# Kernel values of a long convolution written out by group of 32 partitions and gathered in 1-KB runs, in a two-part kernel on one core

## The chip, the core and the metric

The kernel runs on one core of a Trainium2 chip. The metric is the device time of one execution in microseconds (us). Three executions of the kernel before took 1983.52, 1980.21 and 1974.15 us, a median of 1980.21 us. The engines are called as the profile calls them: PE is TensorE, DVE is VectorE, ACT is ScalarE, POOL is GpSimd and SP is SyncE, which here does nothing but issue transfers.

## The reference, cut to what is computed

Two independent computations share the launch; their outputs lie side by side.

```python
# A: attention over 64 segments of 32 rows; 8 memory rows are handed from segment to segment
for s in range(64):
    h = concat([mem, x[32*s:32*s+32]])             # 40 rows of 1024
    q, k, v = h@Wq, h@Wk, h@Wv                     # 32 heads of 128
    o = softmax(mask(q k^T / sqrt(128))) v @ Wo
    mem, out_a[s] = o[:8], o[8:]
# B: a convolution of length 2048 for each of 1024 channels d
K[d, l] = Re sum_n C[d,n] dt[d] B[d,n] exp(dt[d] (A_re + i A_im)[d,n] l)    # 128 states n
y = irfft(rfft(u, 4096) * rfft(K, 4096))[:2048] + u * Dskip
```

Part B needs the kernel values K[d, l] of each channel, then their spectrum, the product with the spectrum of u, and the way back.

## The kernel before, in words

The function `part_b` runs first and `part_a` after it. The order of the work is written by hand (`manual_schedule`): instructions stand on each engine in the order in which the Python code calls them, and an engine waits only for what an instruction needs. Transfers issued from SP and from ACT are counted on eight completion counters in turn, so a transfer also waits until the one eight places ahead of it in the program has landed.

Part B has these stages.

- **Tables, about 65 to 400 us.** Sixteen rounds `f`, each with the same list of words (`ORDER`). A round makes powers of the states on PE, ACT and DVE (`exp_`, `sine`, `products`), multiplies them into kernel values (`values`), and copies these into a tile `KxT` of 128 partitions, 49 columns and 128 channels (`part_out`). Partition 32g+q holds a coarse place q of channel group g, so one channel's values are spread over 32 partitions. Eight rounds fill one half of the 1024 channels (a half has 512, in four groups of 128). Between these words stand pieces of other work: the transform of u on PE, whose result is written to a DRAM tensor `Ud`, and part A's projections of its left rows (`kst` to `PKd`, `vst` to `PVd`, weights into `wsl`). `kst` is one buffer: when its 16 pieces are filled it is written out in eight transfers (L211), and ACT may fill it again (L206) only after that.
- **Rearranging.** The spectrum needs the values as five tiles of 128 places by 512 channels (`ks`). The first half goes from `KxT` to a DRAM tensor `Kd` in 44 transfers (L1079), each of one channel group and one piece of the table `PLACED`. They wait in the list `late`, and `exp_` issues one each time it is called. `load_k` (L1112) loads the five tiles from `Kd` in two transfers in round 15. The second half goes to `Kx1` in one transfer (L1075), at the end of the table stage. It is rearranged by the generator `load_second`: 12 loads straight into the tile `k1` (L1102), 32 copies from DRAM to DRAM into `Kd1` (L1105), and one load of `Kd1` (L1108).
- **Spectra and the way back, about 400 to 620 us.** Sixteen steps `b`, one for each of four frequency blocks of four channel quarters. Step b calls in this order: `times_u(b)` on DVE (four products, L1394); `load_u(b+1)` on SP (two loads of 512 KB from `Ud` into one pair of buffers, L1229, possible only when `times_u(b)` has read them); `spectrum(b+1)` on PE (40 matmuls, L1238), in two halves of 20 into three buffers `hps`; `rotate` and the sums into `Bt` on DVE; one to three loads of weights for part A (L266); in steps 3 to 6 up to twelve transfers of `load_second` each; from step 4 on two inverses on PE (65 matmuls, L1519 and L1513), with an evacuation on ACT (L1534), a store from ACT's queue (L1541) and a load of u (L1477). `spectrum(8)`, called in step 7, is the first to need the second half's tiles in `k1`. An inverse sums two blocks of 256 columns in one PSUM bank, each opened by its own start flag.

Part A then streams weights that do not fit into SBUF (`wst<-WD_...`) through 64 segments.

The few lines around the change that the text needs:

```python
    for _ in range({1: 2, 2: 2, 3: 1, 4: 2, 5: 2, 6: 2, 7: 1, 11: 3, ...}.get(b, 0)):
        next(resident)                       # weights of part A, 512 KB each
    for _ in range(12 if 2 < b < 7 else 0):
        next(second, None)                   # twelve transfers of load_second
    ...
    if b >= 4:
        inverses(2)
```

Of the kernel before, what the change touches and what calls it, by code (L numbers as in the profile page):

```python
# [10 lines left out]
BF16 = mybir.dt.bfloat16  # L11
# [674 lines left out]
NF = NP + NN  # L686
# [16 lines left out]
def part_b(ctx, tc, u, A_re, A_im, B_re, B_im, C_re, C_im, log_dt, Dskip, out_b, ahead, copies, residents, first_state):  # L703
    nc = tc.nc
    L, D = u.shape
# [3 lines left out]
    DH, DQ = 512, 256  # L709
    v, sc, gp, pe, sy = nc.vector, nc.scalar, nc.gpsimd, nc.tensor, nc.sync  # L710

    const = ctx.enter_context(tc.tile_pool(name="b_const", bufs=1))
    dram = ctx.enter_context(tc.tile_pool(name="b_dram", bufs=1, space=bass.MemoryType.DRAM))
    PB = [dram.tile([PARTS[q], D, 128], BF16, name="PB%d" % q) for q in range(2)]
    Ud = dram.tile([4, 4, 128, 4, 2, DQ], F32, name="Ud")
    Kd = dram.tile([641, DH], BF16, name="Kd")
    Kx1 = dram.tile([128, NF * 128], BF16, name="Kx1")
    Kd1 = dram.tile([256, DH], BF16, name="Kd1")
    MId = dram.tile([16, 128, 2, 4, 128], BF16, name="MId")

    ident = const.tile([128, 128], BF16, name="b_ident")
# [7 lines left out]
    XT = ahead.XM_  # L729
# [39 lines left out]
    with tc.tile_pool(name="b_par", bufs=1) as par, tc.tile_pool(name="b_parh", bufs=2) as parh, \  # L769
# [35 lines left out]
        o = 0  # L805
# [154 lines left out]
        for word_ in PAR:  # L960
            word = word_.rstrip("/")
            nm, n_ = word[0], word[1:]
# [83 lines left out]
    KxT = {}  # L1046
# [12 lines left out]
    def part_out(sb, h, kp):  # L1059
# [4 lines left out]
        if sb % 8 == 7 and h == 1:  # L1064
            put_values(sb)

    late = []

    PLACED = ((0, 0, ((8, 1, 32),)), (8, 256, ((8, 2, 16),)), (16, 384, ((4, 1, 4), (8, 4, 8), (40, 1, 4))),
              (24, 512, ((0, 1, 4), (4, 2, 2), (8, 8, 4), (40, 2, 2), (44, 1, 4))))  # L1070

    def put_values(sb):
        kx = KxT["t"]
        if sb // 8:
            late.append(lambda: sy.dma_start(out=Kx1[:], in_=kx[:].rearrange("p j c -> p (j c)")))  # L1075
            return

        def put(out, in_):
            late.append(lambda: sy.dma_start(out=out, in_=in_))  # L1079
        for g in range(4):  # L1080
            dsl = slice(128 * g, 128 * g + 128)
            for p0, u0, cols in PLACED:
                n_j = sum(n for _, _, n in cols)
                dst = Kd[u0:u0 + 8 * n_j, dsl].rearrange("(i j) d -> i j d", j=n_j)
                at = 0
                for j0, js, n in cols:
                    put(dst[:, at:at + n], kx[32 * g + p0:32 * g + p0 + 8, j0:j0 + js * (n - 1) + 1:js, :])
                    at += n
            put(Kd[640:641, dsl], kx[32 * g + 31:32 * g + 32, NF - 1, :])

    def load_second(KT):
        rows = Kx1[:].rearrange("p (j c) -> p j c", j=NF)
        for g in range(4):
            for p0, u0, cols in PLACED:
                n_j = sum(n for _, _, n in cols)
                at, p = 0, 32 * g + p0
                for j0, js, n in cols:
                    src_ = rows[p:p + 8, j0:j0 + js * (n - 1) + 1:js, :]
                    if len(cols) == 1:
                        for lo in range(0, 8 * n_j, 128):  # L1100
                            o = DH * ((u0 + lo) // 128) + 128 * g
                            sy.dma_start(out=KT[:, o:o + 128], in_=src_[lo // n_j:(lo + 128) // n_j])  # L1102
                            yield
                    else:
                        sy.dma_start(out=Kd1[u0 - 384:u0 - 384 + 8 * n_j, 128 * g:128 * g + 128].rearrange("(i j) d -> i j d", j=n_j)[:, at:at + n], in_=src_)  # L1105
                        yield
                    at += n
        sy.dma_start(out=KT[:, 3 * DH:5 * DH].rearrange("p (j d) -> p j d", j=2), in_=Kd1[:].rearrange("(j p) d -> p j d", p=128))  # L1108
# [118 lines left out]
    def load_u(b):  # L1227
        for n_ in range(2):
            sy.dma_start(out=uq[n_], in_=Ud[b % 4, b // 4][:, 2 * n_:2 * n_ + 2].rearrange("p a c d -> p (a c d)"))  # L1229
# [109 lines left out]
    for f in range(16):  # L1339
        if f == 8:  # L1340
            sy.dma_start(out=Dsk[:], in_=Dskip.partition_broadcast(128))
        ahead.burst = 3 if f == 0 else 2
        if f == 0:
            next(others)
        if 1 <= f <= 6:
            next(steps)
        if f == 15:
            for kind, slot in [k for k in pending if k[0] == "P"]:
                run_evict(kind, slot, v.tensor_copy)
            while ahead.late and ahead.late[0]:  # L1350
# [5 lines left out]
            ks = [load_k(XT[:, 0:2048], 0) + load_k(XT[:, 4096:4608], 4)]  # L1356
# [96 lines left out]
    k1 = pool.tile([128, 4096], BF16, name="k1", tag="KT0")  # L1453
# [53 lines left out]
    def products_back(yp, dq, c, neg, mn, kcs):  # L1507
        r, Bt = c // 4, Bs[dq]
        j = r % 2
        for b in range(2):  # L1510
            for kc in kcs:
                if kc == 3 and b == 1 and c % 4 == 2:
                    pe.matmul(yp[:, b, :], lhsT=l4[:, r, :], rhs=w4[:, DQ * dq:DQ * dq + DQ], start=False, stop=False, skip_group_check=True)  # L1513
                for cs in range(2):

                    g_cs = cs if j == 0 else 1 - cs
                    minus = neg is not None and neg[0] <= cs < neg[1]
                    for half, m_, c_ in ((0, MI[c // 2], cs), (1, mn if minus else MI[c // 2], g_cs)):
                        pe.matmul(yp[:, b, :], lhsT=m_[:, b, cs, kc, :], rhs=Bt[:, kc, j, half, c_, :], start=(kc == 0 and cs == 0 and half == 0),  # L1519
                                  stop=(kc == 3 and cs == 1 and half == 1), skip_group_check=True)  # L1520

    def inverse(dq, c, uu, neg, mn):
# [32 lines left out]
    for b in range(16):  # L1555
# [29 lines left out]
            for i in (2 * b, 2 * b + 1):  # L1585
                sy.dma_start(out=MI[i][:], in_=MId[2 * i:2 * i + 2].rearrange("c p a k q -> p c a k q"))
        if b == 2:
            ks.append([k1[:, DH * j:DH * j + DH] for j in range(5)])
            second = load_second(k1[:, 0:2560])
            rows4 = g0[0:4, 5120:6144]  # L1590
            for i in range(4):
                sy.dma_start(out=rows4[i:i + 1, 0:DH], in_=Kd[640:641, :])
                sy.dma_start(out=rows4[i:i + 1, DH:D].rearrange("o (g c) -> o g c", g=4),
                             in_=Kx1[:].rearrange("(g q) f -> q g f", g=4)[31:32, :, 128 * NF - 128:])
            sy.dma_start(out=w4, in_=u[0:4, :])
            gp.tensor_tensor(out=w4, in0=rows4[:, 0:D], in1=w4, op=ALU.mult)
            gp.memset(l4, 0.0)
            gp.memset(l4[:, :, 127:128], float(PLEN / 2))
            gp.affine_select(out=l4[:, :, 127:128], in_=l4[:, :, 127:128], compare_op=ALU.is_ge, fill=0.0, base=0, pattern=[[1, 4], [0, 1]],
                             channel_multiplier=-1)  # L1600
        for _ in range({1: 2, 2: 2, 3: 1, 4: 2, 5: 2, 6: 2, 7: 1, 11: 3, 12: 3, 13: 2, 14: 3}.get(b, 0)):
            next(resident)
        for _ in range(12 if 2 < b < 7 else 0):
            next(second, None)
        if b == 4:
            state = first_state(g0[0:8, 5120:6144], iv.tile([128, 8, 24], BF16, name="xt0", bufs=1))
            next(state)
# [170 lines left out]
```

## Time and profile before

| What | Value |
|---|---|
| Median of three executions | 1980.21 us |
| The profiled execution | 1981.69 us |
| Its span, first to last instruction | 1979.9 us |
| PE busy | 1840.5 us, 93% of the span |
| DVE busy | 1371.1 us, 69% |
| ACT busy | 949.7 us, 48% |
| Mean granted clock of PE | 0.977 |
| Moved by all transfers | 589.91 MB, 298 GB/s on average |

A busy row of the page is a sum over stages that differ: what a change in one stage is worth is read in that stage. The views used here are the page's 40 slices, tables of busy time by stretch of the span (microseconds from the start; "DMA" is the mean busy share of the 16 DMA engines), and the instructions in order of time. In that last view a row gives the start, the duration, the engine, the line, the operation with output and input, and in brackets the idle time of the engine ahead of it and what ended it. "SPq" and "ACTq" rows are the time that a queue needed to issue a transfer, waits for buffers and counters included, and not the transfer itself.

### The profile page before, as it was taken

What the parts mean: (1) busy time and instruction counts of PE and PEld (TensorE: products, weight loads), DVE (VectorE), ACT (ScalarE), POOL (GpSimd) and SP (SyncE); (2) the same over time, 40 slices, a digit from 0 to 9 for tenths busy, and PEclk for the clock granted to TensorE, in tenths of its full rate; (3) what the DMA queues carried; (4) which work ended last, traced back from release to release, by engine and by line L of the source; (5) the groups of instructions that cost most, each with busy time, mean ns of one, the idle gap of its engine ahead of it and who ended that gap; (6) DMA issues with size and microseconds to landing.
All of it is one profiled execution on the core that took longest, in us unless ns stands there. A gap on an engine that the chain in (4) does not pass through costs nothing.

```text
span 1979.9 us, 74693 instructions
## 1 busy us (share of the span) xinstructions
PE 1840.5 (93%) x32006; PEld 1133.3 (57%) x32044; DVE 1371.1 (69%) x3401; ACT 949.7 (48%) x1678; POOL 389.8 (20%) x823
## 2 busy tenths in 40 slices
PE   8999999787998799999999999999999999999999
PEld 3666566456786455555555555555555555555554
DVE  8699999787893466666666666767666666666650
ACT  8799999832123344434444444444434343434330
POOL 2354454212000111111111111111111111111120
PEclk9999999779999799999999999999999999999999
DMA  7989888765478899999999999999999999999991
GB/s 221 255 238 265 264 239 251 210 223 185 144 250 298 312 338 336 351 333 339 340 338 333 348 347 345 350 339 349 340 336 341 337 344 338 344 342 348 328 344 37
DMA packets 329728, 589.91 MB, mean 298 GB/s; under 512 B 87812, under 2 KB 203368, under 8 KB 327220
## 3 DMA queue, kind: packets, MB, share of 16 engines
q1 hardware_dynamic: 277208, 530.64, 78.4%
q10 hardware_dynamic: 45532, 29.57, 4.9%
q0 software_dynamic: 6656, 24.92, 3.4%
q8 instruction: 251, 4.11, 0.9%
q14 instruction: 81, 0.66, 0.1%
HBM read 528.52 MB, written 67.26 MB: 301 GB/s over the span
## 4 chain that ended last, share of the span: by engine, by line
PE 40%; DMA 22%; DVE 3%; ACT 1%; issue 1%; POOL 0%; ACTq 0%; SPq 0%; POOLq 0%; DVEq 0%
PE acc L408 23%; DMA wst<-WD_o 8%; PE pp L521 8%; DMA wst<-WD_v 6%; DMA wst<-WD_k 3%; PE pe L658 3%; PE tr L419 2%; DMA arena<-PKd 2%; DMA wst<-WD_q 1%; DMA out_dram<-arena 1%; PE pv L489 1%; DVE arena L615 1%; PE pv L493 1%; PE sc L433 1%; ACT arena L615 1%
## 5 line engine op out<-in xcount | busy, mean ns | idle before, releaser
L408 PEld LDWEIGHTS <-a_hT 128*32 128x32 bf16 x12352 | 328.2, 96 | 308.8 <-issue 54.0
L414 ACT CAST arena<-acc 128x512 bf16<-128x512 f32 x384 | 225.1, 586 | 395.0 <-PE acc L408 317.6
L521 PEld LDWEIGHTS <-arena 128*32 128x32 bf16 x8256 | 217.0, 96 | 91.0 <-issue 66.4
L408 PE MATMUL acc<-wst,a_hT 128*32 128x512 bf16 x2304 | 229.4, 381 | 24.1 <-DMA wst<-WD_v 16.4
L422 POOL COPY arena<-arena 128x128 bf16<-128x128 bf16 x128 | 37.3, 292 | 842.5 <-DMA arena<-PKd 274.0
L329 DVE TENSOR_SCALAR arena<-keep 128x256 int32<-128x256 int32 (+1 forms) x512 | 175.7, 395 | 31.5 <-PE acc L408 29.1
L408 PE MATMUL acc<-XM,a_hT 128*32 128x512 bf16 x2560 | 185.9, 380 | 0.0
L521 PE MATMUL pp<-W_o,arena 128*32 128x256 bf16 x3584 | 122.6, 274 | 7.3 <-DMA W_o<-in_A_Wo_dram 7.3
L452 ACT ACTIVATE sc<-sc 128x160 f32<-128x160 f32 (+1 forms) x192 | 63.9, 333 | 126.0 <-DVE sc L449 125.5
L448 DVE TENSOR_REDUCE a_mx<-sc 128x4 f32<-128x160 f32 (+1 forms) x192 | 71.7, 373 | 75.0 <-PE sc L436 75.0
L197 PE MATMUL pro<-XM,wsl 128*128 128x512 bf16 x480 | 117.4, 382 | 5.9 <-DVE kst L206 2.2
L408 PE MATMUL acc<-W,a_hT 128*32 128x512 bf16 x1536 | 119.3, 382 | 0.2 <-issue 0.2
L536 DVE COPY arena<-tr 128x512 bf16<-128x512 bf16 x64 | 27.2, 425 | 126.2 <-PE tr L419 126.2
L456 DVE TENSOR_REDUCE a_mx<-sc 128x4 f32<-128x160 f32 (+1 forms) x192 | 72.9, 379 | 55.4 <-ACT sc L452 55.0
L1519 PE MATMUL yp<-Bt,MI 128*128 128x256 bf16 x680 | 105.2, 274 | 0.0
L408 PE MATMUL acc<-g,a_hT 128*32 128x512 bf16 x1024 | 102.2, 381 | 0.0
L1283 DVE TENSOR_SCALAR nr<-ptt 128x456 f32<-128x456 int16 x128 | 80.3, 628 | 29.8 <-PE ptt L1261 26.9
L483 POOL TENSOR_TENSOR arena<-arena,a_BD 128x128 bf16<-128x128 bf16 x128 | 51.0, 399 | 237.8 <-DVE arena L466 222.8
L615 ACT CAST arena<-pp 128x128 bf16<-128x128 f32 x64 | 17.0, 266 | 164.9 <-DVE arena L615 164.9
L1275 ACT ACTIVATE E<-pa 128x648 bf16<-128x648 f32 x128 | 87.8, 713 | 15.8 <-PE pa L1267 13.9
L521 PE MATMUL pp<-wst,arena 128*32 128x256 bf16 x1536 | 76.6, 275 | 19.3 <-DMA wst<-WD_o 17.4
L408 PE MATMUL acc<-wq,a_hT 128*32 128x512 bf16 x1024 | 91.2, 382 | 0.0
(333 smaller groups left out, 4024.4 us busy)
## 6 DMA issues: line engine op xcount, KB each, us to landing
wst<-WD_v SPq DMA_DIRECT2D x256, 512.0 KB
wst<-WD_k SPq DMA_DIRECT2D x192, 512.0 KB
wst<-WD_o SPq DMA_DIRECT2D x192, 512.0 KB
wst<-WD_q SPq DMA_DIRECT2D x128, 512.0 KB
Ud<-ux POOLq DMA_DIRECT2D x16, 1024.0 KB, 8.2
wq<-Ud SPq DMA_DIRECT2D x32, 512.0 KB
wsl<-in_A_Wk_dram SPq DMA_DIRECT2D x16, 512.0 KB
wsl<-in_A_Wv_dram SPq DMA_DIRECT2D x16, 512.0 KB
```

The source lines that it names most:

```text
L197: nc.tensor.matmul(a[:], lhsT=w[:, kc, 128 * j:128 * j + 128], rhs=xTl[:, kc, :, :].rearrange("p s k -> p (s k)"), start=(kc == 0), stop=( ...
L329: nc.vector.tensor_scalar(out=out.bitcast(I32), in0=in_.bitcast(I32), scalar1=0, scalar2=None, op0=ALU.bitwise_or)
L408: nc.tensor.matmul(a[32 * g:32 * g + 32, o_:o_ + rhs.shape[1]], lhsT=hT[:, kc, :], rhs=rhs, start=(kc == 0), stop=(kc == KC - 1), tile_pos ...
L414: nc.scalar.copy(out=q, in_=a[:])
L448: nc.vector.tensor_reduce(out=m_, in_=x, axis=AX.X, op=ALU.max)
L452: nc.scalar.activation(out=flat(sc, i), in_=flat(sc, i), func=ACT.Exp, scale=scale)
L456: nc.vector.tensor_reduce(out=m_, in_=x, axis=AX.X, op=ALU.add)
L521: nc.tensor.matmul(po[32 * qt:32 * qt + 32, o_:o_ + rhs.shape[1]], lhsT=oT[:, h % 4, (h % 16) // 4, :], rhs=rhs, start=False, stop=(h == 3 ...
L658: nc.tensor.matmul(pe[n][:], lhsT=left[2 * b + hi // 16][:, 128 * (hi % 16):128 * (hi % 16) + 128], rhs=wo[u][:, 1024 * hh + 512 * n:1024 ...
L1275: sc.activation(out=T["E", r, e // 4][:, lo:lo + 8 * NE].rearrange("p (i c) -> p i c", i=2), in_=T.pop(("p", r, e))[:, :, 0:4 * NE], func= ...
L1283: v.tensor_scalar(out=T["n", r, e // 4][:, lo:lo + 8 * NT], in0=T.pop(("t", r, e))[:, 0:8 * NT].bitcast(I16)[:, 0:16 * NT:2], scalar1=floa ...
L1519: pe.matmul(yp[:, b, :], lhsT=m_[:, b, cs, kc, :], rhs=Bt[:, kc, j, half, c_, :], start=(kc == 0 and cs == 0 and half == 0), stop=(kc == 3 ...
```

## The change

Both halves now take the same way. A tile `Kx[half]` in DRAM holds 32 places, 49 columns, 4 groups and 128 channels, so that the four groups of one place and column stand side by side as 512 channels (1 KB). `put_values` writes `KxT` there in four transfers, one for each group of 32 partitions (1568 runs of 256 bytes each). Eight copies a half then put the two irregular pieces into a small tensor `Kp[half]`; the first half's are listed in `late` behind 16 empty entries, the second half's in `second`, four issued in step 3 and four in step 4. `load_k` loads each of the five tiles with a transfer of its own, in runs of 1 KB: three straight from `Kx` (32 columns of four places, twice, and every second column of eight places) and two from `Kp`. It is called in round 15 for the first half and in step 6 for the second. The rows of the last place come from `Kx` for both halves. In the inverse only the first block of a bank has a start flag.

In the built program SP issues 58 transfers fewer (34 for both halves in place of 92); the other engines have the same instructions in the same order.

```diff
-    Kd = dram.tile([641, DH], BF16, name="Kd")
-    Kx1 = dram.tile([128, NF * 128], BF16, name="Kx1")
-    Kd1 = dram.tile([256, DH], BF16, name="Kd1")
+    Kx = [dram.tile([32, NF, 4, 128], BF16, name="Kx%d" % i) for i in range(2)]
+    Kp = [dram.tile([16, 16, DH], BF16, name="Kp%d" % i) for i in range(2)]
...
-    PLACED = ((0, 0, ((8, 1, 32),)), (8, 256, ((8, 2, 16),)), (16, 384, ((4, 1, 4), (8, 4, 8), (40, 1, 4))),
-              (24, 512, ((0, 1, 4), (4, 2, 2), (8, 8, 4), (40, 2, 2), (44, 1, 4))))
+    PIECES = ((16, ((4, 1, 4), (8, 4, 8), (40, 1, 4))), (24, ((0, 1, 4), (4, 2, 2), (8, 8, 4), (40, 2, 2), (44, 1, 4))))
     def put_values(sb):
-        kx = KxT["t"]
-        if sb // 8:
-            late.append(lambda: sy.dma_start(out=Kx1[:], in_=kx[:].rearrange("p j c -> p (j c)")))
-            return
...
+        kx, half = KxT["t"], sb // 8
         for g in range(4):
...
+            late.append(lambda g=g: sy.dma_start(out=Kx[half][:, :, g, :], in_=kx[32 * g:32 * g + 32, :, :]))
+        late.extend([lambda: None] * (16 if half == 0 else 0))
+        for p0, cols in PIECES:
+            at = 0
+            for j0, js, n in cols:
+                (late if half == 0 else second).append(lambda p0=p0, at=at, j0=j0, js=js, n=n: sy.dma_start(
+                    out=Kp[half][p0 - 16:p0 - 8, at:at + n, :],
+                    in_=Kx[half][p0:p0 + 8, j0:j0 + js * (n - 1) + 1:js].rearrange("i j g c -> i j (g c)")))
+                at += n
-    def load_second(KT):
...
-    def load_k(KT, lo):
+    def load_k(half, KT, lo):
         n_ = KT.shape[1] // DH
-        sy.dma_start(out=KT.rearrange("p (j d) -> p j d", j=n_), in_=Kd[128 * lo:128 * (lo + n_), :].rearrange("(j p) d -> p j d", p=128))
-        return [KT[:, DH * j:DH * j + DH] for j in range(n_)]
+        ks_ = [KT[:, DH * j:DH * j + DH] for j in range(n_)]
+        for j, t_ in enumerate(ks_):
+            c = lo + j
+            src_ = Kp[half][8 * (c - 3):8 * (c - 2)] if c > 2 else Kx[half][4 * c:4 * c + 4, 8:40] if c < 2 else Kx[half][8:16, 8:40:2]
+            sy.dma_start(out=t_, in_=src_ if c > 2 else src_.rearrange("i j g c -> i j (g c)"))
+        return ks_
...
-                        pe.matmul(..., start=(kc == 0 and cs == 0 and half == 0),
+                        pe.matmul(..., start=(b == 0 and kc == 0 and cs == 0 and half == 0),
...
-        for _ in range(12 if 2 < b < 7 else 0):
-            next(second, None)
+        for _ in range(4 if b in (3, 4) else 0):
+            second.pop(0)()
+        if b == 6:
+            ks.append(load_k(1, k1[:, 0:2560], 0))
```

More of the change, by code (lines that the diff above doesn't have):

```diff
@@ L1065, in part_out @@
             put_values(sb)
-    late = []
-    PLACED = ((0, 0, ((8, 1, 32),)), (8, 256, ((8, 2, 16),)), (16, 384, ((4, 1, 4), (8, 4, 8), (40, 1, 4))),
-              (24, 512, ((0, 1, 4), (4, 2, 2), (8, 8, 4), (40, 2, 2), (44, 1, 4))))
+    late, second = [], []
+    PIECES = ((16, ((4, 1, 4), (8, 4, 8), (40, 1, 4))), (24, ((0, 1, 4), (4, 2, 2), (8, 8, 4), (40, 2, 2), (44, 1, 4))))
     def put_values(sb):
-        kx = KxT["t"]
-        if sb // 8:
-            late.append(lambda: sy.dma_start(out=Kx1[:], in_=kx[:].rearrange("p j c -> p (j c)")))
-            return
-        def put(out, in_):
-            late.append(lambda: sy.dma_start(out=out, in_=in_))
-        for g in range(4):
[L1081 to L1089, printed above, removed]
@@ L1091, in load_second @@
-    def load_second(KT):
[L1092 to L1108, printed above, removed]
@@ L1355, in part_b @@
             uq = [t_[:].bitcast(F32) for t_ in wsl[1:3]]
-            ks = [load_k(XT[:, 0:2048], 0) + load_k(XT[:, 4096:4608], 4)]
+            ks = [load_k(0, XT[:, 0:2048], 0) + load_k(0, XT[:, 4096:4608], 4)]
             load_u(0)
@@ L1518, in products_back @@
                     for half, m_, c_ in ((0, MI[c // 2], cs), (1, mn if minus else MI[c // 2], g_cs)):
-                        pe.matmul(yp[:, b, :], lhsT=m_[:, b, cs, kc, :], rhs=Bt[:, kc, j, half, c_, :], start=(kc == 0 and cs == 0 and half == 0),
+                        pe.matmul(yp[:, b, :], lhsT=m_[:, b, cs, kc, :], rhs=Bt[:, kc, j, half, c_, :], start=(b == 0 and kc == 0 and cs == 0 and half == 0),
                                   stop=(kc == 3 and cs == 1 and half == 1), skip_group_check=True)
@@ L1587, in part_b @@
         if b == 2:
-            ks.append([k1[:, DH * j:DH * j + DH] for j in range(5)])
-            second = load_second(k1[:, 0:2560])
             rows4 = g0[0:4, 5120:6144]
             for i in range(4):
-                sy.dma_start(out=rows4[i:i + 1, 0:DH], in_=Kd[640:641, :])
-                sy.dma_start(out=rows4[i:i + 1, DH:D].rearrange("o (g c) -> o g c", g=4),
-                             in_=Kx1[:].rearrange("(g q) f -> q g f", g=4)[31:32, :, 128 * NF - 128:])
+                for half in range(2):
+                    sy.dma_start(out=rows4[i:i + 1, DH * half:DH * half + DH], in_=Kx[half][31:32, NF - 1].rearrange("i g c -> i (g c)"))
             sy.dma_start(out=w4, in_=u[0:4, :])
```

## The prediction

> **What bounds the kernel now.** I read the page first: the span, the busy row of PE and its slices.
>
> ```profile
> span 1979.9 us, 74693 instructions
> PE 1840.5 (93%) x32006; PEld 1133.3 (57%) x32044; DVE 1371.1 (69%) x3401; ACT 949.7 (48%) x1678; POOL 389.8 (20%) x823
> PE   8999999787998799999999999999999999999999
> ```
>
> PE is the bound over nearly all of the span; the weak slices lie between 350 and 700 us. The stretch in which the second half's values are rearranged (steps 3 to 7) is among them, so the second view is busy time by stretch (PE, PEld, DVE, ACT, POOL, granted clock, DMA share, GB/s).
>
> ```profile
> 445.00:470.00 25.00, 23.74 (x213) 20.24 (x212) 19.10 (x20) 6.56 (x8) 11.21 (x37) 1.00 0.58 182
> 470.00:500.00 30.00, 14.56 (x108) 11.46 (x106) 21.01 (x24) 4.62 (x5) 0.00 (x0) 0.77 0.56 184
> 500.00:540.00 40.00, 40.00 (x351) 34.24 (x350) 31.28 (x36) 9.30 (x10) 0.00 (x0) 0.96 0.51 160
> 540.00:600.00 60.00, 60.00 (x547) 52.40 (x545) 54.80 (x63) 16.29 (x19) 0.00 (x0) 1.00 0.69 215
> ```
>
> From 500 us on, PE is never idle: these steps are PE's own work. From 470 to 500 it works half the time, at a granted clock of 0.77, while no other engine is full and DMA is at 0.56. What PE waits for stands in its instructions in order of time.
>
> ```profile
> 455.90 2.35 PE L1238 MATMUL hps<-XM 128*128 128x256 bf16 x20
> 459.27 2.36 PE L1238 MATMUL hps<-XM 128*128 128x256 bf16 x20 [1.03 <-DVE y L1394]
> ...
> 468.77 2.35 PE L1238 MATMUL hps<-XM 128*128 128x256 bf16 x20
> 474.88 3.38 PE L1238 MATMUL hps<-XM 128*128 128x256 bf16 x20 [3.76 <-DVE y L1394]
> ...
> 486.04 0.49 PE L1238 MATMUL hps<-k,g 128*128 128x256 bf16 x3
> 498.22 6.68 PE L1238 MATMUL hps<-k,g 128*128 128x256 bf16 x37 [11.68 <-DMA k<-Kd]
> ...
> 512.04 4.53 PE L1238 MATMUL hps<-k,XM 128*128 128x256 bf16 x40
> ...
> 523.71 4.53 PE L1238 MATMUL hps<-k,XM 128*128 128x256 bf16 x40
> ```
>
> The starts are those of spectrum(6) at 455.90, (7) at 468.77, (8) at 486.04, (9) at 512.04 and (10) at 523.71. A step without waits is 523.71 - 512.04 = 11.67 us. The three steps from spectrum(6) to spectrum(9) took 56.14 us and hold 3 x 11.67 = 35.01 us of work: 21.1 us are lost. 1.03 + 3.76 + 11.68 = 16.5 of them are waits; the other 4.6 are matmuls at a lower clock behind a wait (37 matmuls in 6.68 us at 498.22, against 40 in 4.53).
>
> Who makes PE wait is read on SP, ACT and DVE in the same stretch.
>
> ```profile
> 444.89 7.06 SPq L1105 DMA_DIRECT2D Kd<-Kx  x8
> 452.63 0.89 SPq L1229 DMA_DIRECT2D wq<-Ud  x2
> 456.16 7.08 SPq L1105 DMA_DIRECT2D Kd<-Kx  x8
> 466.64 1.14 SPq L1229 DMA_DIRECT2D wq<-Ud  x2
> 470.49 8.15 SPq L1105 DMA_DIRECT2D Kd<-Kx  x8
> 485.17 0.81 SPq L1229 DMA_DIRECT2D wq<-Ud  x2
> 495.41 0.38 SPq L1108 DMA_DIRECT2D k<-Kd  x1
> ```
>
> ```profile
> 482.44 1.31 ACTq L1541 DMA_DIRECT2D out_dram<-uu  x2
> ```
>
> ```profile
> 445.14 1.21 DVE L1394 TENSOR_TENSOR y<-wq,hps 128x1024 f32<-128x1024 f32 x1
> 451.04 2.36 DVE L1469 TENSOR_TENSOR Bt<-y 128x1024 bf16<-128x1024 f32 x2
> 456.87 1.22 DVE L1394 TENSOR_TENSOR z<-wq,hps 128x1024 f32<-128x1024 f32 x1 [3.47 <-DMA wq<-Ud]
> 472.47 1.22 DVE L1394 TENSOR_TENSOR z<-wq,hps 128x1024 f32<-128x1024 f32 x1 [4.59 <-DMA wq<-Ud]
> 489.51 1.22 DVE L1394 TENSOR_TENSOR z<-wq,hps 128x1024 f32<-128x1024 f32 x1 [6.03 <-DMA wq<-Ud]
> ```
>
> In step 4 DVE has read the first u buffer at 446.35, but SP issues load_u(5) only at 452.63: its queue is full of the twelve rearranging transfers. DVE, done with Bt at 453.40, waits until 456.87. Step 5 repeats it (466.64). In step 6 load_u(7) at 485.17 waits for the counter of an output store that ACT issued at 482.44, late because PE was late. Then load_k's last load goes out at 495.41, behind eight more copies, and PE restarts at 498.22. So one chain, from SP's queue over load_u and DVE to PE, makes all three waits.
>
> **The change part by part.** *Second half, steps 3 to 6 (the gain).* 45 transfers become 13: four copies in step 3, four in step 4, none in step 5, five loads in step 6. SP's 7 to 8 us of copies ahead of each load_u go. Step 4: load_u(5) goes out at about 446.4 and 448.6; a load_u took 456.87 - 452.63 = 4.24 us from issue to use, so it is there by 452.9 and DVE goes on at 453.4. A step on DVE without waits is 11.0 us (456.87 to the end of Bt at 467.87), less than PE's 11.67, so times_u(6) starts at 464.4 and times_u(7) at 475.4; the two halves of the u buffers are free 8.7 and 6.5 us ahead of each of these, and a load is there 4.24 us after its issue. PE then starts spectrum(7) at 467.6, (8) at 479.2, (9) at 490.9: all 21.1 us, if `k1` is full at 479.2.
>
> *The loads of `k1` in step 6.* They follow load_u(7) (466.7, 468.9) and two weight loads in SP's queue, from about 470.3. I let transfers land in the order of their issue: load_u(7) at 473.2, two weights of 512 KB at 474.8 and 476.4, 640 KB at 478.4, with 1.6 us for 512 KB from the 321 GB/s of the row 400 to 405 below. That is 0.8 us ahead of need. If each of the five loads cost 4.24 us one after the other, the last lands at 491.5: 12.3 us of waiting, and 2.5 of low clock as at 498.22. The term is between 0 and 14.8; I take 1.0, by the sum, whose rows are the nearest (256 KB went from issue to use in 498.22 - 495.41 = 2.8 us).
>
> The Trainium skill (DMA: Bandwidth & Descriptors, "Why a DMA increments its semaphore by 16 and not by 1") says that a transfer uses the largest number of engines up to 16 that divides the slowest dimension of both sides. By it the two loads from four places would run on 4 of the 16 engines and the third on 8; as an estimate the last would land 2.8 us later, and the wait would be 2.0 in place of 1.0. No view here shows engines one by one.
>
> *The dumps.* Prices of transfers in short runs, and of the old contiguous dump:
>
> ```profile
> L1105 SPq DMA_DIRECT2D Kd<-Kx x32: 609/610/1349, 444.9 to 493.2; - x32
> ...
> L160 SPq DMA_DIRECT2D VXd<-PVd x16: 527/1114/3729, 123.1 to 382.4; - x16
> ```
>
> ```profile
> 370.19 13.08 SPq L160 DMA_DIRECT2D VXd<-PVd  x8
> ```
>
> ```profile
> 280.70 2.17 SPq L1079 DMA_DIRECT2D Kd<-KxT  x2
> ```
>
> ```profile
> 400.00:405.00 5.00, 5.00 (x28) 3.33 (x27) 3.37 (x4) 1.53 (x3) 0.00 (x0) 0.56 0.94 321
> ```
>
> A copy of 16 to 64 runs costs SP 0.610 us whatever its runs, and one of 1024 runs as little as 0.527. Eight of 1024 runs of 256 bytes took 13.08 us, 1.6 ns a run, so four dumps (6272 runs) take 10.0 us; the old second dump, 1.6 MB, took about 5 at 321 GB/s.
>
> ```profile
> 240.06 7.27 SPq L1079 DMA_DIRECT2D Kd<-KxT  x2
> ...
> 275.25 1.01 SPq L211 DMA_DIRECT2D PKd<-kst  x2
> ```
>
> ```profile
> 250.00:255.00 5.00, 4.75 (x98) 3.09 (x92) 4.65 (x9) 4.37 (x7) 4.17 (x5) 1.00 0.51 131
> 255.00:260.00 5.00, 4.88 (x101) 4.05 (x100) 4.54 (x8) 4.97 (x6) 3.96 (x6) 1.00 0.62 154
> ```
>
> ```profile
> 282.91 0.59 ACT L206 CAST kst<-pro 128x512 bf16<-128x512 f32 x1
> ```
>
> ```profile
> 399.79 0.32 SPq L1075 DMA_DIRECT2D Kx<-KxT  x1
> ```
>
> ```profile
> 418.25 1.21 DVE L1394 TENSOR_TENSOR z<-wq,pa 128x1024 f32<-128x1024 f32 x1
> ```
>
> First half, from 240 us: behind the dumps stand the eight PKd transfers, the last issued by 276.26 and landed, at 2.8 us, by 279.1; ACT refills `kst` at 282.91, so 3.8 us are free. DMA has 2.45 + 1.9 = 4.35 us idle from 250 to 260. 10.0 - 4.35 - 3.8 = 1.85 us late; 6.2 if the idle time can't be used, 0 if the removed copies make room. I take 1.5; a late ACT there is a late end, since ACT is full there. Second half, from 399.8: dumps 10.0, two loads of MI about 1.7, load_u(2) 4.24: 415.7, against need at 418.25. Cover of 2.5 us; 0.5 taken, 0 to 3.
>
> *The rest.* The eight copies of the first half replace 44 in the table stage and are covered by PE, ACT and DVE, busy 4.4 to 5.0 of each 5 us in the rows from 250 to 260. Start flags: the same matmuls, nothing. The first half's load_k keeps its place in round 15, ahead of two loads of u and of all the building of the spectrum's matrices; I take nothing for its three more transfers. Behind step 8 every wait moves along with PE.
>
> **Sum.** 21.1 - 1.0 - 1.5 - 0.5 = 18.1 us less. The profiled execution took 1981.69 us (1979.9 of span), so 1963.6; it is 1.5 above the median of the three runs, 1980.21, so 1962.1 for the median, 0.9% faster.
>
> **The rivals.** *The wait for `k1` stays*: the loads pass one after the other, and PE waits 12.3 us at spectrum(8) again. For it: they stand behind load_u(7) and two weight loads, and the fourth and fifth wait for their counters. Against: 2.8 us for 256 KB. 21.1 - 14.8 - 2.0 = 4.3 us gained, 1975.9: no change.
>
> *The dumps cost their upper ends*, 6.2 and 3: 21.1 - 1.0 - 9.2 = 10.9, 1969.3, at the edge.
>
> *Slower: SP pays for a dump by the run.* The pair at 280.70 took 2.17 us for 384 runs, 5.65 ns a run; 6272 runs would hold SP 35 us. At 240 us all but the 7.27 us of the two issues that go and the 3.8 of slack delay ACT; at 399.8 all but 12.5 delays DVE. Loss: 12544 runs times the price, less 23.6: 47.3 us at 5.65 ns, so 1980.2 - 20.1 + 47.3 = 2007. It decides from 3.5 ns a run. Against it: the flat 0.610 us, and 1.6 ns at L160; the pair's time holds a wait for a counter.
>
> *The copies weren't what held load_u*, and the time stays at 1980: the queue's rows speak against it (in steps 4 and 5 load_u follows the copies and loads within SP's next rows, after DVE has long freed its buffer). Less than 0.02, held within the third case.
>
> **How the numbers follow.** Forecast 0.70 (1957 to 1968, from terms near their lower ends and the scatter of runs); upper ends of the dumps 0.10; the wait for `k1` stays 0.10; slower 0.10. 0.5% (9.9 us) is about what a measurement of this kernel can tell from no change; the second case falls half on either side. Faster 0.75, same 0.15, slower 0.10. The range 1957 to 1973 leaves out the last two cases.
>
> **What would show it.** Right: PE full from 455 to 600 us, spectrum(9) starting some 20 us earlier, no DVE wait on `wq<-Ud` in steps 5 and 6, load_u within 1 us of DVE's last read. Wrong: PE idle over 5 us ahead of `hps<-k` (the loads), ACT idle ahead of `kst` near 283 us, DVE idle ahead of 418, or dump rows on SP of 5 us and more where DMA isn't full.

## The result and the profile after

The changed kernel takes 1960.99 us (median of six runs, 1958.09 to 1965.35); six runs of the kernel before, among them the three that the prediction had, give 1979.78 us. The ratio is 0.9915 with a 95% interval of 0.9887 to 0.9944: 0.6 to 1.1% faster, 11 to 22 us. The forecast was 1962.1.

The page of the changed kernel, the same three lines as before:

```profile
span 1958.4 us, 74636 instructions
PE 1841.3 (94%) x32006; PEld 1132.2 (58%) x32044; DVE 1368.9 (70%) x3401; ACT 949.0 (48%) x1678; POOL 390.8 (20%) x823
PE   8999999889998899999999999999999999999998
```

PE does the same work in a span shorter by 21.5 us; the tenth slice (441 to 490 us), a 7 before, is a 9. Busy time by stretch (PE, PEld, DVE, ACT, POOL, granted clock, DMA share, GB/s) in the changed kernel:

```profile
445.00:470.00 25.00, 25.00 (x215) 21.52 (x213) 24.29 (x25) 3.18 (x5) 15.42 (x50) 0.94 0.92 311
470.00:500.00 30.00, 28.02 (x234) 23.36 (x233) 27.01 (x31) 8.60 (x9) 0.00 (x0) 0.94 0.74 228
```

From 470 to 500 us PE works 28.0 of 30 us, where it worked 14.6, and the granted clock there is 0.94 in place of 0.77. PE's instructions of the spectrum, in order of time:

```profile
461.84 4.53 PE L1215 MATMUL hps<-XM 128*128 128x256 bf16 x40
473.51 4.53 PE L1215 MATMUL hps<-XM 128*128 128x256 bf16 x40
485.18 0.27 PE L1215 MATMUL hps<-k,g 128*128 128x256 bf16 x1
486.28 0.27 PE L1215 MATMUL hps<-k,g 128*128 128x256 bf16 x1 [0.83 <-DMA k<-Kx]
487.37 0.61 PE L1215 MATMUL hps<-k,g 128*128 128x256 bf16 x2 [0.82 <-DMA k<-Kx]
488.24 5.76 PE L1215 MATMUL hps<-k,g 128*128 128x256 bf16 x36 [0.26 <-DMA k<-Kp]
501.13 4.53 PE L1215 MATMUL hps<-k,XM 128*128 128x256 bf16 x40
```

Spectrum(6) starts at 461.84, (7) at 473.51, (8) at 485.18, (9) at 501.13. The first two steps take 11.67 us each, the step without waits. The third still waits 1.9 us for the loads of `k1`, and its matmuls are slower behind that (36 in 5.76 us; the granted clock is 0.70 from 488.3 to 494 us). I call S the time from spectrum(6) to spectrum(9): 56.14 us before, 39.29 here. SP's queue in the same steps:

```profile
448.38 3.29 SPq L1078 DMA_DIRECT2D Kp<-Kx  x4
451.78 2.44 SPq L1206 DMA_DIRECT2D wq<-Ud  x2
455.29 3.05 SPq L1078 DMA_DIRECT2D Kp<-Kx  x4
461.95 1.59 SPq L1206 DMA_DIRECT2D wq<-Ud  x2
472.23 2.60 SPq L1206 DMA_DIRECT2D wq<-Ud  x2
475.83 3.95 SPq L1089 DMA_DIRECT2D k<-Kx  x3
480.46 1.76 SPq L1089 DMA_DIRECT2D k<-Kp  x2
```

Three u loads go out at 451.78, 461.95 and 472.23, at PE's pace. Ahead of them SP now waits for DVE, which is still reading the buffers (SP's waits from 440 to 515 us: in total, times, longest):

```profile
SPq L1206 <- DVE y L1371: 18.0, 5, 6.2
```

What DVE waits for them from 440 to 600 us, first before, then after (us in total, times, longest):

```profile
DVE z L1394 <- DMA wq<-Ud: 17.2, 4, 6.0
```

```profile
DVE z L1371 <- DMA wq<-Ud: 0.8, 1, 0.8
```

Yet spectrum(9) starts only 10.9 us earlier (501.13 against 512.04), not S's 16.9: spectrum(6) itself starts 5.9 us later (461.84 against 455.90). 3.3 of these are there from the first cast of `KxT` on (102.70 against 99.40), long before the first transfer that the change touches, which SP issues at 243.30. They are still 3.3 at the first row below (259.39 against 256.09), behind the four dumps; that cast stands between 256.07 and 260.38 in the profiles of the other kernels, so such an offset is scatter. The first half then loses 3.4 us, and 0.8 us come back between 296 and 462 us. Two casts of `KxT` that enclose the loss, on DVE, before and after:

```profile
256.09 0.57 DVE L1063 CAST KxT<-kp 128x392 bf16<-128x392 f32 x1
...
289.28 0.55 DVE L1063 CAST KxT<-kp 128x392 bf16<-128x392 f32 x1
```

```profile
259.39 0.57 DVE L1062 CAST KxT<-kp 128x392 bf16<-128x392 f32 x1
...
274.91 0.55 DVE L134 COPY xst<-pt_x 128x768 bf16<-128x768 bf16 x1
280.38 0.57 DVE L1062 CAST KxT<-kp 128x392 bf16<-128x392 f32 x1 [2.26 <-PE kp L1054]
295.97 0.56 DVE L1062 CAST KxT<-kp 128x392 bf16<-128x392 f32 x1
```

I call F the time between them: 289.28 - 256.09 = 33.19 us before, 295.97 - 259.39 = 36.58 after: 3.4 us lost, and not by the wait of ACT ahead of `kst` that the prediction had there: in this profile ACT doesn't wait for it. DVE waits for PE, and PE (first row) for ACT (second row, the eviction it names):

```profile
279.62 0.21 PE L1054 MATMUL kp<-gr 128*32 128x49 bf16 x4 [2.17 <-ACT vst L191]
```

```profile
279.01 0.57 ACT L191 CAST vst<-pro 128x512 bf16<-128x512 f32 x1
```

This `kp` has no use for `vst`. In the built program the reason is seen: the pool of this tile draws on PSUM banks 5, 6 and 7, and which one a tile gets is settled when the kernel is built, by the order in which the planner expects tiles to come free. In the kernel before this `kp` gets bank 6, last used by `pt_x`; in the changed one it gets bank 7, which holds the projection that PE has just computed, and must wait until ACT has evicted it. The wait itself is 2.2 us; the rest of the 3.4 is slower matmuls behind it, at a granted clock of 0.61 from 280 to 284 us, where the kernel before has 1.00. (e11_small below has the same wait, keeps a clock of 1.00 behind it, and loses 2.2 us only.) With the dumps in SP's queue the planner places DVE's copy out of `pt_x` behind that eviction. On the chip the copy is done at 275.46 (the row at 274.91), 4.2 us before `kp` starts: bank 6 was free. All engines but SP have the same instructions in the same order in both kernels; from this tile on 124 of the pool's 303 tiles stand in other banks.

The second half's dumps, on SP:

```profile
406.26 5.46 SPq L1073 DMA_DIRECT2D Kx<-KxT  x4
...
415.74 0.88 SPq L1206 DMA_DIRECT2D wq<-Ud  x2
```

and the instruction on DVE that stands at 418.25 in the kernel before:

```profile
424.60 1.21 DVE L1371 TENSOR_TENSOR z<-wq,pa 128x1024 f32<-128x1024 f32 x1
```

The dumps start 6.47 us later than the old one did (399.79) and this instruction 6.35: they cost nothing. 5.46 us for 6272 runs is 0.87 ns a run. The first half's four dumps took SP 12.7 us (9.48 for the two at 243.30, 3.20 for the two at 255.10), 2.0 ns a run, where DMA is full (a share of 1.04 to 1.08 from 243 to 253 us). Either ends the rival in which SP pays 3.5 ns or more.

The third part of the span, R, runs from spectrum(9) to the end: 1979.9 - 512.04 = 1467.9 us before, 1958.4 - 501.13 = 1457.3 after. No instruction of it changed.

### The profile page after: what moved, and what is told of

The parts are those of the page before. It is cut to its first block, busy times and chain, and to the rows that moved or that the text cites. A ratio compares the mean times of both kernels' runs of the same rounds, so it can differ in the third digit from the quotient of the medians.

```text
span 1958.4 us, 74636 instructions
## 1 busy us (share of the span) xinstructions
PE 1841.3 (94%) x32006; PEld 1132.2 (58%) x32044; DVE 1368.9 (70%) x3401; ACT 949.0 (48%) x1678; POOL 390.8 (20%) x823
## 4 chain that ended last, share of the span: by engine, by line
PE 38%; DMA 23%; DVE 5%; issue 1%; ACT 1%; POOL 0%; DVEq 0%; SPq 0%; POOLq 0%; ACTq 0%
PE acc L408 21%; DMA wst<-WD_v 9%; PE pp L521 8%; DMA wst<-WD_o 5%; DMA wst<-WD_k 4%; PE pe L658 3%; DMA arena<-PKd 2%; PE tr L419 2%; DMA wst<-WD_q 2%; PE pv L493 1%; PE pv L489 1%; DVE arena L474 1%; PE sc L433 1%; DVE arena L615 1%; DVE arena L471 1%
## 5 line engine op out<-in xcount | busy, mean ns | idle before, releaser
L419 PEld LDWEIGHTS <-arena 128*128 128x128 bf16 x1024 | 57.5, 98 | 52.2 <-issue 44.7
```

The source lines that it names most:

```text
L419: nc.tensor.transpose(out=p[:, hl, :, :].rearrange("p a b -> p (a b)"), in_=q[:, 128 * hl:128 * hl + 128], identity=ident[:])
```

## The experiments

All kernels in one table; F, S and R are read as above, from one profile each; medians and ratios (95% interval) are against runs of the kernel before on the same chip, whose medians were 1978.0 to 1979.8.

| kernel | F | S | R | median us | ratio |
|---|---|---|---|---|---|
| before | 33.19 | 56.14 | 1467.9 | 1979.8 | |
| changed | 36.58 | 39.29 | 1457.3 | 1961.0 | 0.9915 (0.9887-0.9944) |
| e1_flag | 33.18 | 54.23 | 1466.8 | 1981.1 (one run) | |
| e2_behind | 33.18 | 57.40 | 1458.5 | 1976.0 | 1.0007 (0.9983-1.0032) |
| e3_second_only | 33.27 | 36.63 | 1463.6 | 1959.2 | 0.9907 (0.9871-0.9943) |
| e4_first_only | 36.58 | 53.65 | 1466.5 | 1981.9 | 1.0008 (0.9982-1.0033) |
| e5_lead4 | 39.55 | 35.81 | 1455.3 | 1964.1 | 0.9936 (0.9911-0.9961) |
| e6_k_step5 | 36.46 | 35.01 | 1463.0 | 1961.1 | 0.9911 (0.9883-0.9938) |
| e7_both | 40.28 | 35.01 | 1469.0 | 1963.4 | 0.9931 (0.9906-0.9956) |
| e9_act | 33.18 | 43.03 | 1466.6 | 1978.1 | 0.9990 (0.9969-1.0012) |
| e11_small | 35.41 | 70.91 | 1459.8 | 1996.2 | 1.0093 (1.0058-1.0128) |
| e10_lead20 | 33.17 | 35.00 | 1464.7 | 1959.0 | 0.9911 (0.9884-0.9938) |
| after_again | 36.59 | 36.21 | 1460.7 | 1962.2 | 0.9926 (0.9899-0.9954) |
| e12_again | 33.18 | 35.01 | 1465.8 | 1958.2 | 0.9897 (0.9863-0.9931) |

The kernel e12_again is that of e10_lead20 and after_again the changed one, both run once more on one chip. R goes from 1455 to 1469 us with no order that follows the edits: 1465.3 is the mean of the five profiles with the second half as before, 1462.4 that of the eight with the changed one (e11_small left out). So one profile's total is good to some 7 us, and a cause of 3 or 4 us is read from F and S.

### Is it SP's order?

The kernel before with the copies of a step behind load_u:

```diff
         if 0 < b < 15:
             load_u(b + 1)
+        for _ in range(12 if 2 < b < 7 else 0):
+            next(second, None)
...
-        for _ in range(12 if 2 < b < 7 else 0):
-            next(second, None)
```

> The kernel before with one edit: the twelve rearranging transfers of a step are issued right behind load_u(b+1) and no longer ahead of it; not one of the 45 transfers is dropped. Queue theory (the copies' place in SP's order held load_u): load_u(5) and load_u(6) go out within 1 us of DVE's last read, DVE's 17.2 us of waits on wq<-Ud in steps 4 to 6 go, spectrum(6) to spectrum(9) falls from 56.14 us to 36 to 41 (the k loads stay at the end of the list), so 15 to 20 us less, 1960 to 1965. Rival, transfer theory (the short runs themselves keep the DMA engines or the counters, and load_u is late wherever it stands): spectrum(6) to spectrum(9) stays over 50 us and the time within 5 us of 1980. Whichever of the two holds also tells how much of the change's gain came from having fewer transfers: with the queue theory almost none.

A miss: S 57.40 us, ratio 1.0007. SP's queue in that kernel shows why:

```profile
451.21 0.98 SPq L1229 DMA_DIRECT2D wq<-Ud  x2
452.23 1.20 SPq L1102 DMA_DIRECT2D k<-Kx  x2
453.47 8.25 SPq L1105 DMA_DIRECT2D Kd<-Kx  x8
461.76 1.11 SPq L1102 DMA_DIRECT2D k<-Kx  x2
462.92 1.86 SPq L266 DMA_DIRECT2D W<-in_A_Wq_dram  x2
464.82 0.44 SPq L1730 DMA_DIRECT2D xt<-VXd  x1
465.37 0.30 SPq L1731 DMA_DIRECT2D g<-in_A_mem_dram  x1
465.71 0.91 SPq L1477 DMA_DIRECT2D uu<-in_B_u_dram  x2
467.42 2.31 SPq L1229 DMA_DIRECT2D wq<-Ud  x2
```

From load_u(5) to load_u(6) are 16.2 us. The first eight rows take 15.05 of them, and the twelve copies 10.6. These rows hold 2.7 us in which SP waits until earlier loads of `Ud` and of weights have landed, so that their completion counters are free; what is left, 12.3 us, is still more than PE's step of 11.67 us. Wherever in the step the copies stand, SP can't get through it in time. But the run doesn't yet part "SP's time" from "short transfers are slow", so two more did: the same 45 transfers from another queue, and more issues without bytes.

### SP's time or the transfers?

```diff
     def load_second(KT):
...
-                        sy.dma_start(out=Kd1[...], in_=src_)
+                        sc.dma_start(out=Kd1[...], in_=src_)
```

(all of `load_second`'s calls alike)

> The kernel before with all 45 rearranging transfers of the second half issued by ACT in place of SP; same places in the program, same bytes, same runs. Theory, SP's time (the twelve copies, two u loads, weights and input rows of a step need more of SP than a step of 11.67 us has, so moving copies behind load_u could not help): load_u goes out on time, DVE's waits on wq<-Ud go, spectrum(6) to spectrum(9) falls from 56.1 us to 36 to 44 (ACT is 12 to 13 us busy of 60 here, so 7 to 9 us of issue a step still fit, perhaps not without a wait ahead of k), 1960 to 1968. Rival, transfers (the short runs or the chain of counters hold the data however they are issued): over 52 us, and 1975 to 1982.

The changed kernel with small transfers added:

```diff
         for _ in range(4 if b in (3, 4) else 0):
             second.pop(0)()
+        for i in range(12 if 2 < b < 7 else 0):
+            sy.dma_start(out=Kz[12 * b - 36 + i:12 * b - 35 + i, :], in_=Kx[1][31:32, NF - 1, 0, :])
```

> The changed kernel with twelve more transfers at the end of each of steps 3 to 6, of one run of 256 bytes each, that write to a scratch nobody reads: almost no bytes, only issues in SP's queue. Theory, SP's time: load_u is late again in steps 4 to 6, DVE waits for wq<-Ud by 2 to 6 us a step and PE ahead of spectrum(8) for the k loads; spectrum(6) to spectrum(9) goes from 39.3 us to 48 to 58, and the time to 1970 to 1979. Rival, transfers (bytes and short runs count, not issues): the stretch stays at 39 to 41 us and the time at 1961.

e11_small decides between bytes and number. Its 48 transfers carry 12 KB in all; SP spends on them (a group of twelve a row):

```profile
449.33 8.74 SPq L1581 DMA_DIRECT2D Kz<-Kx  x12
462.93 11.83 SPq L1581 DMA_DIRECT2D Kz<-Kx  x12
479.17 11.29 SPq L1581 DMA_DIRECT2D Kz<-Kx  x12
494.60 12.75 SPq L1581 DMA_DIRECT2D Kz<-Kx  x12
```

and PE waits in the old places, first for DVE's `y` (behind load_u), then for `k1`:

```profile
485.21 3.65 PE L1216 MATMUL hps<-XM 128*128 128x256 bf16 x20 [8.65 <-DVE y L1372]
513.68 0.39 PE L1216 MATMUL hps<-k,g 128*128 128x256 bf16 x1 [17.52 <-DMA k<-Kx]
```

S grows from 36.2 to 39.3 us to 70.9, worse than with the 45 larger transfers of the kernel before, and the time to 1996: the way that the theory had it, but far more than the 48 to 58 us and 1970 to 1979 that I expected. SP's waits tell a part of it: 13.8 us go, ahead of these 48 transfers, until loads and output stores eight places earlier have landed and their counters are free. One transfer of 256 bytes holds SP for (shortest, median, longest, in ns)

```profile
L1581 SPq DMA_DIRECT2D Kz<-Kx x48: 467/587/2479, 449.3 to 506.8; - x48
```

where a copy of 16 to 64 runs held it 610. So what a step pays for is the number of transfers and not their bytes: 0.6 us of issue for each, and the waits for counters that each brings with it. No run here parts these two. The Trainium skill (DMA: Bandwidth & Descriptors, "Issuing engines are not separate DMA queues") says that issuing from several engines saves only the time to start a transfer, usually small beside the transfer itself; here, with 12 KB in all, it isn't small.

e9_act is a half hit. With the copies off SP, S falls to 43.03 us, inside what was expected, but the time stays (0.9990). Waits of that kernel from 425 to 530 us (us in total, times, longest):

```profile
ACT mn L1485 <- DMA Kd<-Kx: 17.8, 2, 9.7
DVE z L1394 <- DMA wq<-Ud: 8.6, 2, 6.7
PE hps L1238 <- DVE y L1394: 7.9, 2, 5.5
PE yp L1519 <- ACT mn L1485: 6.1, 2, 3.2
```

Now ACT's own `mn` stands behind the copies, PE's inverse waits for `mn`, and two of the three steps last 16.6 and 14.7 us. SP isn't free either: since both queues share the eight counters, its u loads (L1229), weights (L266) and input rows (L1477) wait 15.5 us in the same stretch until copies that ACT issued have landed. S fell by 13.1 us, but the stretch ahead of it, from the end of F to spectrum(6), grew by 6.0 (spectrum(5) waits 5.49 us for DVE's `y`), and the profiled span is 6.4 us shorter. Why the median is only 0.5 us lower isn't settled.

### Which half

e3_second_only takes the kernel before and gives it the second half of the change (dumps by group, eight pieces, five loads); e4_first_only gives it the first half. The edits are the respective hunks of the diff, with the old code kept for the other half.

> The kernel before with the second half of the change alone (four group dumps at 400 us, eight pieces, five loads; the first half by its old 24 transfers). In the built program every PSUM tile stands where it does in the kernel before. Theory (the gain is all in the second half, through SP's issues, and the first half's dumps only cost): the offset to the kernel before stays constant from 240 to 425 us, spectrum(6) to spectrum(9) 35.8 to 39.3 us in place of 56.1, so 16 to 20 us less than before, 1959 to 1964. Rival, the first half matters too (its 16 fewer transfers ahead of 300 us): only 10 to 14 us of the gain remain, 1966 to 1970.

> The kernel before with the first half of the change alone. The PSUM banks are those of the changed kernel. Theory: 3 us lost between 270 and 290 us by the wait of kp for ACT's eviction (2.2 us) and slower matmuls behind it, everything after as in the kernel before, spectrum(6) to spectrum(9) 56 to 58 us: 1981 to 1984. Rival, the first half gains by its fewer transfers: 1970 to 1976.

Both times are as the theory had them: the second half alone gives all of the gain (0.9907), the first half alone nothing (1.0008, with F 36.58 and the same 2.2 us of `kp` behind `vst`). (The first half's old transfers are 44, not the 24 of the text above.) The start flags alone are e1_flag, whose F and R are those of the kernel before. Its S, 54.23, and that of e4_first_only, 53.65, lie below the 56 to 58 that I expected: in S both run the instructions of the kernel before, so S of the old second half scatters by 2.5 us.

> The kernel before with the start flags of the changed kernel alone (one opening flag for the two sums of a bank). Same matmuls in the same order on every engine: no part of the time changes, 1970 to 1987 like the runs of before; spectrum(6) to spectrum(9) 56 to 58 us. Rival: if the second flag cost PE a stop, each of the inverse steps from 600 us on would be shorter.

### The 3.4 us of the first half, and the loads of `k1`

```diff
+        late.extend([lambda: None] * (4 if half == 0 else 0))
         for g in range(4):
...
-        late.extend([lambda: None] * (16 if half == 0 else 0))
+        late.extend([lambda: None] * (12 if half == 0 else 0))
```

> The changed kernel with the four dumps of the first half four places later in the list of late transfers (four empty places ahead of them, twelve behind them where there were sixteen), so that the eight pieces stay where they are. In the built program only five places of SP's order differ, and the PSUM bank of a kp tile in the same round goes back to the one that the kernel before has (in the changed kernel that tile stands in the bank that a projection has just filled, so its matmuls wait for ACT's eviction: 2.17 us at 279.62). Bank theory: that wait goes, and the stretch from the cast of KxT at 259.4 to the product gr at 287.8 falls from 28.4 us to the 25.1 us of the kernel before; 3.3 us less than the changed kernel, 1957.7. Rival, dump theory (the prediction's: the dumps' bytes make the PKd stores and what waits for them late): the same bytes pass in the same 20 us, and the 3.3 us stay: 1961. Spectrum(6) to spectrum(9) stays at 39.3 us in both.

Half a miss. With the banks of the kernel before, `kp`'s wait for `vst` is gone, as the bank theory says. But F is 39.55, longer still: four places later the dumps hold the PKd stores, and ACT waits for them ahead of `kst`, which is the very mechanism of the prediction:

```profile
290.25 0.59 ACT L206 CAST kst<-pro 128x512 bf16<-128x512 f32 x1 [5.74 <-DMA PKd<-kst]
```

Both mechanisms exist, then. `kp` waits for `vst` in every kernel that has it in bank 7 (the changed one in both profiles, e4_first_only, e6_k_step5, e11_small) and in none that has it in bank 6; ACT waits for PKd by 5 us and more only where the dumps stand four places later. In the changed kernel ACT's `kst` has no wait there, but it seems that the first wait covers a part of the second. The last of its PKd stores has landed at 288.21 (the last increment of its counter in the trace). Without the bank's wait `kst` would stand 3.3 us behind the 282.91 of the kernel before, at 286.21, and ACT would wait some 2.0 us: an estimate from these rows, which no run tests. Even the transfers of the kernel before leave little slack there: they have landed 0.03 us before `kst` in its profile, 0.9 to 1.3 in those of e1_flag, e2_behind and e9_act, and e3_second_only, which has the old first half too, has ACT waiting for them (us in total, times, longest):

```profile
ACT kst L206 <- DMA PKd<-kst: 0.6, 1, 0.6
```

```diff
-        if b == 6:
+        if b == 5:
             ks.append(load_k(1, k1[:, 0:2560], 0))
```

> The changed kernel with the five loads of the second half's values called at the end of step 5 and not of step 6, so that they stand ahead of load_u(7) in SP's queue. Theory: the three waits of PE ahead of spectrum(8) (0.83, 0.82 and 0.26 us) and the slower matmuls behind them go; spectrum(6) to spectrum(9) falls from 39.29 to 35.0 to 35.5 us: 4 us less, 1957. Rival: the loads then stand ahead of load_u(7) and hold it, as the copies did before: DVE waits for wq<-Ud in step 6 by 1 to 4 us, the stretch stays at 37 to 40 us, and nothing is gained: 1959 to 1962.

S is 35.01 us to the hundredth, three steps of 11.67, as the theory had it for PE. But the rival's sign is there too. Counted from spectrum(6), the first three loads go out 11 us earlier than in the changed kernel, the last two only 4.7: ahead of the fourth SP waits 8.5 us until an output store has landed and its counter is free. So load_u(7) goes out at 477.08, and DVE waits 3.1 us for it. PE doesn't feel that: no matmul of these three steps waits. The total is that of the changed kernel, since 1 to 4 us lie within what R scatters.

> The changed kernel with both edits: dumps of the first half four places later, the five loads at the end of step 5. If both theories hold, their gains add, since they lie in different stages: 3.3 + 4.0 = 7.3 us less than the changed kernel, 1953.7, 1.3% below the kernel before. If the dump theory holds in place of the bank theory: 1957. If the loads hold load_u(7): 1958. If neither edit helps: 1961.

S 35.01, F 40.28 (ACT ahead of `kst` 6.0 us): the two edits act where e5 and e6 put them, so the sum expected fell with e5.

```diff
+        late.extend([lambda: None] * (20 if half == 0 else 0))
         for g in range(4):
...
-        late.extend([lambda: None] * (16 if half == 0 else 0))
+        late.extend([lambda: None] * (8 if half == 0 else 0))
...
-        if b == 6:
+        if b == 5:
```

> The changed kernel with the first half's four dumps twenty places later in the list of late transfers (eight empty places behind them), behind the PKd stores, and the five loads of the second half at the end of step 5. In the built program every PSUM tile stands in the bank that it has in the kernel before. Theory of two costs in the first half (2.2 us of wait by the bank plus the slow matmuls behind it in the changed kernel; 5.7 to 6.0 us of ACT waiting for PKd's stores where the dumps stood four places later): neither appears, and the offset to the kernel before stays constant from 240 to 350 us, 3.3 us less than the changed kernel; spectrum(6) to spectrum(9) 35.0. Together 7 us less than the changed kernel: 1953 to 1955. Rival, the dumps cost 3 us or more of DMA wherever they stand: the offset grows by 3 to 6 us between 285 and 350, 1957 to 1961.

> The changed kernel itself once more, beside the next one on the same chip: 1958 to 1965, with 3.3 us lost between 270 and 290 us, and spectrum(6) to spectrum(9) between 35.8 and 39.3 us.

> The kernel with the dumps twenty places later and the five loads at the end of step 5 once more, beside the changed kernel on the same chip. By the stages (3.3 us in the first half, 0.8 to 4.3 us at the five loads) it should lie 4 to 7.6 us below the changed kernel, 1953 to 1958. Rival: what is gained before 640 us is absorbed by the stage behind it, whose DMA share is 0.95 to 0.97, and both kernels agree within 2 us.

With the dumps behind the PKd stores and the old banks neither wait appears (casts of `KxT`, e10_lead20):

```profile
258.95 0.57 DVE L1062 CAST KxT<-kp 128x392 bf16<-128x392 f32 x1
...
292.12 0.55 DVE L1062 CAST KxT<-kp 128x392 bf16<-128x392 f32 x1
```

F is 33.17 and S 35.00 us. The four dumps, issued at 294.73 to 308.86, fall behind F; from the end of F to spectrum(6) are 165.7 us, against 166.6 in the kernel before, so they cost nothing there. That is all these two edits can give, 4.6 to 7.7 us in F and S beside the two profiles of the changed kernel. The totals don't show it in full: 1959.0 and 1958.2, where 1953 to 1955 and 1953 to 1958 were expected. On one chip the medians are 1958.2 and 1962.2 (ratios 0.9897 and 0.9926, whose intervals overlap): the direction fits, the runs don't prove it.

## Why the prediction was right, step by step

*What bounds the kernel now.* Right in the chain (SP, load_u, DVE, PE) and in its size: with no wait left S is 35.01, so 21.1 us were there to be had in the profile of before (19.2 in e1_flag's and 18.6 in e4_first_only's, which run the same stage). "Its queue is full of the twelve rearranging transfers" holds in a sharper form: not their place ahead of load_u but their number, 10.6 us of SP, waits for counters included, in a step of 11.67 us.

*Second half, minus 21.1.* Measured, with the next term in it: 56.14 - 39.29 = 16.9 and 56.14 - 36.21 = 19.9 us in the two profiles. Load_u(6) went out at 461.95, 1.0 us after DVE's last read of the buffer, as foreseen.

*The loads of `k1`, plus 1.0.* Inside the bounds of 0 to 14.8, but undersized: S - 35.01 is 4.3 and 1.2 us in the changed kernel, 0.8 and 1.6 in e5_lead4 and e3_second_only, with the same five loads in the same place. The waits alone were 1.9 us in the profile shown; the matmuls at a low clock behind them, which the prediction had counted for the old wait, were left out of this one. Its sum had the last load landed at 478.4, which is 484.3 in this profile (spectrum(6) is 5.9 us later); PE got it at 488.24. PE used the second and third load 9.8 and 9.7 us after their issue, and the fourth and fifth went out only after waits of 0.65 and 1.10 us for counters, as the rival had it. The rule weighed there (2.0 in place of 1.0; the Trainium skill, DMA: Bandwidth & Descriptors, "Why a DMA increments its semaphore by 16 and not by 1") isn't decided: waits from 0.2 to 1.9 us agree with it and without it.

*First half's dumps, plus 1.5.* This step failed, in its mechanism and in a figure of its own. It cost 3.4 us, by a PSUM bank that the build chose anew, and no row of the kernel before could price that. And the 3.8 us that it took as free ahead of `kst` weren't there: it let the last PKd store land 2.8 us after its issue, at 279.1, but in the trace of the kernel before the store issued at 275.68 has landed only at 282.88, 0.03 us before ACT fills `kst` again. With that its sum gives 10.0 - 4.35 = 5.65 us in place of 1.85. The mechanism named, PKd late and ACT ahead of `kst`, came out where the dumps stood four places later: ACT waits 5.7 and 6.0 us, and F is 6.4 and 7.1 us longer, at and over the upper bound of 6.2.

*Second half's dumps, plus 0.5.* 0, within 0 to 3: nothing behind them moved. *Start flags and pieces, 0*: nothing to be seen of either.

*The sum.* F and S together give 16.9 - 3.4 = 13.5 and 19.9 - 3.4 = 16.5 us against the 18.1 of the prediction. The medians differ by 18.8, with an interval of 11 to 22 that holds all of these. So the forecast's hit to one microsecond owes 2 to 5 us to scatter. That behind step 8 every wait moves along with PE can't be told from R, which differs by up to 14 us between profiles.

*The rivals.* The wait for `k1` (1975.9) and SP paying by the run (2007) are ruled out by the 1.2 to 4.3 us measured and by 0.87 to 2.0 ns a run; the first half's upper end of "the dumps cost their upper ends" is what e5_lead4 and e7_both had.

## What to carry to other kernels

Count the transfers of a queue against the step that it serves: twelve more, at about 0.6 us of issue each, took SP 8.7 to 12.8 us of a step of 11.67 us, waits for counters included, however small they were. Moving them within the step or onto an engine with its own in-order work didn't help here; fewer and larger ones did. An edit of transfers alone can also change which PSUM bank a tile gets, so compare the built programs tile by tile before a few microseconds are put down to DMA. And read such microseconds from a stage with fixed ends, not from the total.

## What the runs showed of the hardware that was not expected

A transfer of 256 bytes held SP's queue 587 ns (median of 48), as long as one of 16 to 64 runs (610 ns); issued by ACT the same copies took 623 to 672 ns. The four dumps of 1568 runs each took SP 0.87 ns a run where DMA isn't full (a share of 0.69 from 406 to 412 us) and 2.0 ns where it is. A store of `kst` issued at 275.68 landed 7.2 us later, where the prediction had taken 2.8. A wait of 2.2 us of PE behind the eviction of a bank cost 3.4 us where the granted clock fell to 0.61 behind it, and 2.2 us where it stayed at 1.00. That such a wait stands at all agrees with the Trainium skill (Perfetto Trace Analysis, "Matmuls"), which lets independent groups rotate through different banks so that an eviction overlaps the next group.
